# A written-out plan of 1175 operations drawn up anew: orders, engines and slots of a fused attention and gMLP kernel

## The chip, the cores and the metric

The kernel runs on one core of one Trainium2 chip. The core has a matrix engine (TensorE, PE in the profile; its weight loads are PEld), a vector engine (VectorE, DVE), an activation engine (ScalarE, ACT), a general engine (GpSimd, POOL) and a sequencer that issues transfers (SyncE, SP). Each engine works through its own list of instructions in order; semaphores make one wait for another. The metric is the time of one execution on the device in microseconds. The median of three runs is given, and one execution has been recorded by the hardware profiler.

## The reference, cut to what matters

```python
def _A_ref(x, wqkv, wo):          # S = 2048 rows, D = 448, H = 16 heads of 28, window W = 256
    q, k, v = ...                 # x @ wqkv, split in heads
    scores = jnp.einsum('bhqd,bhkd->bhqk', q, k) * Dh ** (-0.5)
    mask = (idx[:, None] - idx[None, :] >= 0) & (idx[:, None] - idx[None, :] < W)
    p = _softmax(jnp.where(mask[None, None], scores, -1000000000.0), axis=-1)
    return jnp.einsum('bhqk,bhkd->bhqd', p, v) ... @ wo

def _B_ref(x, w_in, w_sp, b_sp, w_out):
    z = _gelu(jnp.einsum('bsd,df->bsf', x, w_in))          # 1792 columns
    z1, z2 = z[..., :Fh], _layernorm(z[..., Fh:])          # Fh = 896
    g = jnp.einsum('ts,bsf->btf', w_sp, z2) + b_sp[None, :, None]
    return jnp.einsum('bsf,fd->bsd', z1 * g, w_out)

sa, ca, ga, sb, cb, gb = ...                               # silu(c) @ w_mod, six rows of 448
h = _layernorm(x) * (1 + ca) + sa
x = x + ga * _A_ref(h, A_wqkv, A_wo)
h = _layernorm(x) * (1 + cb) + sb
x = x + gb * _B_ref(h, B_w_in, B_w_sp, B_b_sp, B_w_out)
```

Everything is bf16; sums of products are kept in float32.

## The kernel before, in words

The 2048 rows are 16 tiles of 128 rows, in four blocks of four tiles. All data stays in on-chip memory between the load of x and the store of the result. The work is described as 1175 operations. An operation is one instruction, or for PE a short run of matmuls into the same bank of PSUM, or one transfer. Each has the engines that may do it (`ways`), the operations that it depends on (`deps`), and the buffers that it takes (`take`): a slot of a small rotating buffer or one of eight PSUM banks.

Nothing is scheduled while the program is built. The string PLAN holds one word per operation, in one order for all engines. In the word `a402.5` the letter names the engine (p PE, a ACT, d DVE, t POOL, s SP), the number the operation, and what follows the slots that it takes. `Sched.order` reads the words one after another. Each engine's own list is its words in that order; whoever takes a slot waits for all users of what held it before. Then the semaphores are counted and the waits written in front of the instructions. So PLAN alone says which engine does an operation, what stands ahead of it on that engine, and which buffer it has to wait for.

The stages, with the lines that the text names:

- **Start.** x and the first weights are loaded by SP and ACT (L395, L398, L404, L408). PE forms c's column (L515) and the rows sa and ca (L545, words p45 to p48); DVE copies them to modT (L574, L575, words d85 and d86). The 36 matmuls of L564 are fillers on a constant tile whose result nobody reads. For the first block the layer norm is statistics (L628, L630, DVE), the power of the variance (L632, POOL) and xn (L643, DVE; words d116, d117 for the first two tiles). PE transposes xn (L739), and DVE or ACT moves it out of PSUM to hT, multiplied and shifted by modT (L748 is ACT's form, L750 DVE's; words 126, 127, 129, 130 for the first two tiles). WQK is a padded copy of the weights of q and k in eight parts (L616 on DVE or POOL, L617 on ACT; word d106 is one).
- **Later blocks.** xn is made by DVE or POOL (L643, or L648 and L650), SP issues one transposing transfer per tile (L465, hT<-xn; words s193 to s196 for the second block), and hT is multiplied and shifted in place (L731).
- **Projections.** L796, L820 and L762 form q and k from WQK, L840 forms v; they are moved out of PSUM by ACT (L801, L771, L832, L844) or DVE (L802, L772, L833, L845). q is also copied into a block-diagonal tile QBD, in pieces (L814, L789 on ACT; L815, L790 on DVE). Operation 217 is the first L820 of the second block.
- **Attention of tile j.** Scores (L925 for the first two tiles, then L955 and L966), exponentials on ACT (L911), masks by multiplication on DVE (L974, L995), products with v (L1002), the reciprocal of the sum and its product on DVE (L1016, L1018), a transposing transfer (hT<-o_sb), the product with wo (L1028, scaled by POOL or DVE in L600) and the sum with x (L1032, DVE). Operation 775 is an L1002 of the last tile but one.
- **Second layer norm.** L628, L630, L632, L643 or L648 and L650, a small copy (L655, L656), a transposing transfer (hT<-xn, the second use of that name) and the multiplication (L1051 on ACT, L1053 on DVE or POOL).
- **gMLP.** L1122 and L1143 are the products with w_in, with gelu on ACT (L1129, L1151), z2 is normalized (L628, L630, L632, then L1134 on DVE). L1167 is the product with w_sp, 28 groups of 16 matmuls of 512 columns: each is followed by an addition on DVE (L1171) and a product on POOL (L1174). L1186 is the product with w_out, L1196 the sum with x on DVE, L1201 the store. w_sp comes in by 32 transposing transfers (wspA, wspB).

Inside an engine's list nothing overtakes. A transfer waits at the head of SP's list for its input, and everything behind it in that list waits as well.

The lines that turn a word into a place on an engine and a buffer:

```python
for at, word in enumerate(PLAN.split()):
    n, *slots = map(int, word[1:].split("."))
    op = self.ops[n]
    for h, k in zip(op.take, slots):
        h.slot = h.res.options[k]
        for u in h.slot:
            old = h.res.last[u]
            if old is not None:
                op.deps.update(old.until)
            h.res.last[u] = h
    op.eng = names[word[0]]
    self.prog[op.eng].append(op)
```

Of the kernel before, what the change touches and what calls it, by code (L numbers as in the profile page):

```python
# [15 lines left out]
d126 d127 d120 d121 d118 d119 a107 p83.1 p80.0 p81.1 p79.2 p77.0 p55.3 p72.2 p71.0 s12 d183 d181 p65.1 t104  # L16
p54.0 p149.1 p84.2 p140.5 p141 p150 a151 p82.1 p57.2 a142 t109 t110 t108 p137.7 p138 a139 p66.2 t122 d124.2
d123.0 p134.3 p131.6 p69.3 p56.0 p146.0 p147 p61.2 a132 d177 d184 d135 a136 s13 d243 d179 d178 d182 d180 t28
t185 t191 t187 t189 d245 d44 d241 d186.3 s11 p143.7 p370.0 a133 p164.1 p171.6 p172 d244 p165 d166 a148 p152.0
p144 d145 d173 d247 p153 d154 a371.0 p376.0 p155.1 p156 d157 a42 a377.4 p394.0 a395.1 a396 a170 t39 d380 d372  # L20
d246 d167 d374 p158.7 p159 a160 s15 p93.1 p94 d95 d248 d87 d88 d242 d397 p96.0 p97 d98 d378 s193 t188.1 s194
t190.2 s195 t192.0 s196 d197 d200 p401.0 a402.5 p174.1 p175 a176 p161.7 p162 p373.0 p89.0 p90 d91 d198 d92
a403 a43 p421.0 a422.6.0 t249 t253 d404 t251 t199 p375 p379 p381 d406 d382 d399 t252.2 d163 p217.0 p218 a219
a169 p210.1 p211 d212 p429.0 a430.0 p201.0 p202 a203 d168 p204.1 p205 a206 s14 d309 d383.2 p398.0 p400 p448.0
a449.2.1 s16 d426 s831 s258 t254.1 s259 d250.0 d255 d425 d432 d311 s384 s257 t256.3 s260 t100 t99 t261 t102
t262 t264 p226.0 p423.0 a424 p207.1 p227 p405 p208 d228 d305 p407 d408 d409.1 d306 s410 d101 d310 d431 a209
d215 d453 p456.0 p229.0 a457.1 d459 d214 d458 d452 p220.1 p221 p230 a231 p427.0 p428 s833 p475.0 p433 p434
d435 p223.0 p224 d225 d312 p450.0 a222 p232.1 d436.2 s437 d213 a476.3.2 d480 p483.0 d307 p233 d234 p235.0 p236
a451 a216 p477.0 p454.0 p455 a484.0 p501.0 d485 d486 d308 s21 s17 s834 p460 p461 d462 d479 d463.0 s464 a237
t263 p385.0 p386 d387 p411.1 p412 a478 p503.0 d413 t313 a502.6.0 p528.0 a504 d388 d505 d389 p481.0 p482 p487  # L30
p488 p271.0 p530.0 d489 d490.1 a529.2.1 d533 d506 d532 p272 a273 p509.0 a510.5 p268.1 p274.0 p275 d276 p269
d270 p507.0 p508 a531 p555.0 a556.3.2 p281.0 p265.1 p266 a267 d512 p282 p557.0 a558 a283 d511 p513 t317 t318.1
s323 t319 t320.2 s324 d314.0 s321 t315 t316.3 s322 t328 d279 d414 d560 p536.0 a537.1 p438.1 p439 d440 d280
p514 d515 d516.0 p287.0 p288 a289 p290.1 p291 a292 p563.0 a564.5 p238.0 p239 d278 p293.1 p534.0 p294 p535
p582.0 a240 p465.0 p466 d441 d442 d538 d415 d277 s20 s491 s830 s517 t390 d539 d391.2 t392 s393 a295 a583.4.0
d559 p540 p541 p284.1 p584.0 p285 a286 p590.0 a591.2 d566 d467 p299.0 p300 a301 d542 d543.1 p561.0 p562 d586
d565 d468 p567 p568 p608.0 t416 t327 t325 d326 d587 p518.1 p335.0 p519 d569 d570.0 p588.0 a585 p589 p336 d593
# [10 lines left out]
d578 t579.2 d746 d655 p721.0 p722 p727 p750.0 a751.4 p728 d747 d729 d730.1 s731 p360.1 p361 p625.0 p744.0 p626
p769.0 d752 d627 d753 d628 a362 p748.0 p679.1 p680 d681 a745 p749 p754 p755 d756 d757.2 p771.0 a770.6.0 p777.0
a772 p706.1 p707 p732.0 p733 d773 d774 p775.0 p776 t580 s581 t809 a778.1 p852.0 p853.1 p854 d656 d708 d734  # L50
d779 d682 d780 d808 t604 d605.0 s758 p759.0 p760 d761 p781 p782 d783 d784.0 a856 d629 t630 t631 p855 a862
p868.3 p869.2 p870 p871 a878 a872 p980.0 p981.1 p982 p983 a986 a987 d735 d736 t657 t658 t606 t659.2 d857 d683
t810 t807 p884.3 p885.2 p886 p887 d709 d710 d632.1 d762 d763 d879 d633 s369 s825 s785 s826 s607 t684 d685 s634
a984 a985 p900.0 p901.1 p902 p903 t737 t711 t660 d686.0 t687 a894 d895 d896 t764 a888 p996.3 p997.2 p998 p999
s661 d712.1 d858 d738 s688 s840 s824 s823 a904 p988.0 d905 a814 a910 p989.1 p990 a1000 a1001 a1003 a992 a1002
a993 p786.0 t799 t797 t713 t811 t813 t801 t812 d765 d889 t766.0 d859 d863 d874 d906 s714 d864 t767 s768 d907
t739.2 d897 d912 t898 d865 d880 d890 p787 d788 d740 s741 s832 p991 a995 d789 d790 t791 d873 d911 d875 t792
d793.1 p932.2 a994 p933.0 p934 p935 a936 d937 p916.1 p917.3 a942 d944 d938 d943 d913 p918 a920 d922 p919 a926
p1004.0 p1005.1 p1006 p1007 a1011 a1009 a1010 a1008 t860 t794 s795 t818 d817 t816 d891 d815 d881 d939 d927
d899 d928 d945 t914 t876 d877 d921 t908 d909 t882 d923 p948.2 p949.3 p950 p951 p964.1 p965.0 p966 a952 d929  # L60
d953 d954 a958 d959 d955 d883 d960 t892 t956 d893 t940 p967 a968 a974 p1028.3 p1029.1 p1030 p1031 t866 t930
t946 t924 t800 a1032 a1033 p1012.2 p1013.3 p1014 a1034 p1020.0 a1035 p1021.1 p1022 p1015 a1017 a1016 a1018
a1025 p1023 a1026 a1027 a1019 a1024 d976 d961 d970 d975 d969 d977 d931 d971 t978 d861 d915 d925 d941 d947 d979
d867 s828 s822 s827 s829 s820 s844 s821 s851 s845 s850 t972 d973 d957 t962 d963 p1087.4 p1051.5 s819 p1036.1
d1037.1 d1088.0 t1038 p1048.2 p1090.4 t1089 p1042.7 d1043.0 t1044 d1049.0 t1050 p1081.3 d1082.0 t1083 s839
s836 s838 s849 s841 s843 s846 s837 s847 s842 s848 p1123.7 p1072.2 d1124.0 d1052.1 t1053 t802 t796 t1125
p1120.0 d1121.1 t1122 p1084.7 d1085.1 t1086 p1156.3 d1157.1 t1158 d1073.1 t1074 d1091.1 p1078.6 p1138.7
d1079.0 t1080 t1092 p1045.4 p1039.6 d1046.1 p1153.1 t798 t1047 d1040.0 t1041 d1139.0 p1075.6 p1114.2 p1054.4
p1141.0 p1150.7 d1055.1 t1056 d1076.1 p1060.4 p1147.6 t1077 p1096.5 t1140 d1154.0 p1144.1 d1061.3 d1115.1
p1093.2 d1097.0 t1155 d1145.0 p1102.3 p1063.1 p1057.4 t1146 d1142.0 s1098 d1103.0 t1116 p1105.5 s1062 d1151.1  # L70
d1094.3 t1152 d1058.2 s1059 d1148.1 t1149 d1106.1 t1107 p1069.4 d1070.1 s1071 d1064.1 s1095 s1065 p1108.7
p1117.5 p1111.0 d1109.1 t1110 d1112.1 t1143 p1167.2 p1066.1 t1113 p1163.4 d1118.0 t1119 s1104 d1067.0 s1068
p1168 d1169.0 s1170 p1171.0 p1172 d1173.2 s1174 p1126.3 p1129.6 d1130.0 d1127.1 s1128 s1131 p1159.5 p1160
p1164 d1161.3 s1162 p1099.2 d1165.0 d1100.2 s1101 s1166 p1132.5 d1133.3 s1134 p1135.3 d1136.1 s1137
# [1194 lines left out]
```

## Time and profile before

| | us |
|---|---|
| median of three runs | 277.24 |
| lowest and highest | 277.05, 278.53 |
| the profiled execution | 277.96 |
| its span on the core | 276.2 |
| PE, DVE, ACT, POOL busy | 268.5, 163.7, 121.5, 118.1 |

The profile gives each instruction's start and length on each engine. Busy is the part of a stretch in which at least one instruction of the engine runs. A group of instructions is named by its line, its engine, its operation and what it writes and reads; "us, mean ns" is the time of all and of one. A wait is named by the group that waited and the group that ended it, with the sum, the number and the longest. The chain is found by following back, from the last instruction, what released each step. The granted clock is 1.00 at full speed and 0.50 at half.

### The profile page before, as it was taken

What the parts mean: (1) busy time and instruction counts of PE and PEld (TensorE: products, weight loads), DVE (VectorE), ACT (ScalarE), POOL (GpSimd) and SP (SyncE); (2) the same over time, 40 slices, a digit from 0 to 9 for tenths busy, and PEclk for the clock granted to TensorE, in tenths of its full rate; (3) what the DMA queues carried; (4) which work ended last, traced back from release to release, by engine and by line L of the source; (5) the groups of instructions that cost most, each with busy time, mean ns of one, the idle gap of its engine ahead of it and who ended that gap; (6) DMA issues with size and microseconds to landing.
All of it is one profiled execution on the core that took longest, in us unless ns stands there. A gap on an engine that the chain in (4) does not pass through costs nothing.

```text
span 276.2 us, 8403 instructions
## 1 busy us (share of the span) xinstructions
PE 268.5 (97%) x3751; PEld 155.1 (56%) x3751; DVE 163.7 (59%) x365; ACT 121.5 (44%) x142; POOL 118.1 (43%) x160
## 2 busy tenths in 40 slices
PE   7999998999999899999999999999999999999995
PEld 5976686678677676544444444444444444454552
DVE  3799999979899989939789301221212022153143
ACT  2599998899899689476766500000000000000000
POOL 7565467626574231498258003254453023062320
PEclk9999999999999799999999999999999999999999
DMA  7999744845442533658499996000000000001013
GB/s 206 316 221 189 96 101 114 107 96 110 114 63 61 107 60 61 176 114 141 97 155 191 213 182 135 0 0 0 2 0 0 0 2 0 33 17 63 0 39 116
DMA packets 67301, 25.54 MB, mean 92 GB/s; under 512 B 58497, under 2 KB 66178, under 8 KB 67266
## 3 DMA queue, kind: packets, MB, share of 16 engines
q1 hardware_dynamic: 66304, 24.21, 43.8%
q10 hardware_dynamic: 962, 0.80, 1.1%
q8 instruction: 29, 0.48, 0.8%
q14 instruction: 6, 0.05, 0.1%
HBM read 9.01 MB, written 1.84 MB: 39 GB/s over the span
## 4 chain that ended last, share of the span: by engine, by line
PE 78%; DVE 13%; DMA 4%; POOL 1%; SPq 1%; issue 1%; DVEq 0%
PE ps L1167 35%; PE ps L1122 8%; PE ps L1143 8%; PE ps L1186 8%; PE ps L1002 5%; DVE PT L974 4%; PE ps L1028 4%; PE ps L955 3%; DMA x_sb<-in_A_x_dram 3%; PE ps L820 3%; PE ps L762 2%; DVE st_all L628 2%; PE ps L840 2%; DMA hT<-xn 2%; DVE o_sb L1018 1%
## 5 line engine op out<-in xcount | busy, mean ns | idle before, releaser
L1174 POOL TENSOR_TENSOR z1T<-tmpg,z1T 128x512 bf16<-128x512 bf16 x28 | 32.0, 1153 | 77.2 <-DVE tmpg L1171 77.2
L1171 DVE TENSOR_TENSOR tmpg<-ps,bsp_bc 128x512 bf16<-128x512 f32 x28 | 19.0, 689 | 76.0 <-PE ps L1167 64.7
L911 ACT ACTIVATE PW<-ps 128x2048 bf16<-128x2048 f32 (+1 forms) x42 | 59.9, 1451 | 6.1 <-PE ps L955 4.5
L1167 PE MATMUL ps<-wspB,z 128*128 128x512 bf16 x224 | 50.1, 379 | 0.0
L1167 PE MATMUL ps<-wspA,z 128*128 128x512 bf16 x224 | 49.5, 379 | 0.0
L632 POOL TENSOR_TENSOR rs_all<-mv_all,neghalf 128x1 f32<-128x1 f32 (+2 forms) x37 | 24.1, 672 | 34.3 <-DVE mv_all L630 34.3
L974 DVE TENSOR_TENSOR PT<-PW,mask 128x1024 bf16<-128x1024 bf16 x56 | 38.0, 702 | 0.2
L1167 PEld LDWEIGHTS ps<-wspA,z 128*128 128x128 bf16 x224 | 21.8, 98 | 26.6 <-issue 0.4
L1167 PEld LDWEIGHTS ps<-wspB,z 128*128 128x128 bf16 x224 | 21.9, 98 | 26.2
L1002 PE MATMUL ps<-Vaug,PT 128*128 128x32 bf16 x496 | 23.3, 177 | 1.4 <-DVE o_sb L1018 1.4
L1002 PEld LDWEIGHTS ps<-Vaug,PT 128*128 128x128 bf16 x496 | 21.4, 96 | 4.3 <-DVE o_sb L1018 2.2
L1122 PE MATMUL ps<-w_in,hT 64*128 64x448 bf16 x224 | 22.0, 350 | 0.0
L1186 PE MATMUL ps<-w_out_g,z1T 128*128 128x448 bf16 (+2 forms) x119 | 22.0, 342 | 0.0
L1143 PE MATMUL ps<-hT,w_in 64*128 64x512 bf16 x196 | 22.0, 376 | 0.0
L628 DVE BATCH_NORM_STATS2 st_all<-z 128x6 f32<-128x448 bf16 x32 | 18.4, 606 | 5.8 <-ACT z L1129 5.8
L628 DVE BATCH_NORM_STATS2 st_all<-x_sb 128x6 f32<-128x448 bf16 x32 | 19.4, 615 | 2.9 <-DMA x_sb<-in_A_x_dram 2.7
L1002 PE MATMUL ps<-Vaug,PW 128*128 128x32 bf16 x224 | 19.7, 177 | 0.0
L820 PE MATMUL ps<-hT,WQK 112*128 112x128 bf16 x256 | 17.9, 223 | 1.6 <-DVE KT L833 1.1
L1151 ACT ACTIVATE z1T<-ps 128x512 bf16<-128x512 f32 x28 | 14.6, 603 | 9.1 <-PE ps L1143 9.1
L1196 DVE TENSOR_TENSOR fin<-ps,x_sb 128x448 bf16<-128x448 f32 (+2 forms) x17 | 9.8, 595 | 14.7 <-PE ps L1186 9.9
L1002 PEld LDWEIGHTS ps<-Vaug,PW 128*128 128x128 bf16 x224 | 17.6, 96 | 1.1
L1129 ACT ACTIVATE z<-ps 128x896 bf16<-128x896 f32 x16 | 13.9, 913 | 7.9 <-PE ps L1122 5.4
(105 smaller groups left out, 354.1 us busy)
## 6 DMA issues: line engine op xcount, KB each, us to landing
out_dram<-fin SPq DMA_DIRECT2D x15, 112.0 KB, 1.7
wmodB<-in_w_mod_dram SPq DMA_DIRECT2D x1, 1568.0 KB, 15.0
x_sb<-in_A_x_dram SPq DMA_DIRECT2D x3, 448.0 KB, 8.0
w_in<-in_B_w_in_dram SPq DMA_DIRECT2D x3, 448.0 KB, 4.5
w_out_g<-in_B_w_out_dram SPq DMA_DIRECT2D x1, 784.0 KB, 4.7
bsp_bc<-in_B_b_sp_dram SPq DMA_DIRECT2D x1, 512.0 KB, 5.1
x_sb<-in_A_x_dram SPq DMA_DIRECT2D x2, 224.0 KB, 4.8
hT<-xn SPq DMA_TRANSPOSE x28, 3.2
```

Of the source, the lines that this page charges most:

```text
L628: st = [dve(0.62, lambda e, t=t, o=12 - 6 * (n - ci), s=s: e.bn_stats(st_all[:, slot, t, o:o + 6], s()), deps(t), prio) for ci, s in enume ...
L632: return pool(0.4 + 0.15 * len(tiles), lambda e: e.tensor_tensor(rs_all[:, slot, a:b], mv_all[:, slot, a:b, 1], neghalf[:, 0:b - a], ALU.pow),
L820: km = lambda g, kc, start, stop, h=h, t=t: lambda e: e.matmul(ps[:, h.slot[0], g * 128:(g + 1) * 128], lhsT=WQK[0:CP, kc, 16 + 4 * g:20 + ...
L911: ex = act(xdur, lambda e, out_ap=out_ap, in_ap=in_ap: e.activation(out_ap(), in_ap(), ACT.Exp, scale=SCALE), [s] + list(after), v - 8.0 + ...
L974: return lock_d(0.68, lambda e: e.tensor_tensor(cols(hp.slot[0] * 2048 + 1024 * k, [[256, 4], [128, 2], [1, 128]]), cols(at_w() + pad + at ...
L1002: fns.append(lambda e, hp=hp, hO=hO, hi=hi, bi=bi, kb=kb, hd=hd, nb=nb, a=at[hi][bi], p_of=p_of: e.matmul(ps[:, hO.slot[0], 32 * hd:32 * h ...
L1122: return lambda e, kc, p0, start, stop: e.matmul(ps[:, hs[t % 2].slot[hf], 0:D], lhsT=hT[p0:p0 + 64, kc, t * 128:(t + 1) * 128], rhs=w_in[ ...
L1143: return lambda e, kc, p0, start, stop: e.matmul(ps[:, hs[b // 2].slot[b % 2], :], lhsT=w_in[p0:p0 + 64, kc, ft * 128:(ft + 1) * 128], rhs ...
L1167: m = pe(16 * MMS, [lambda e, h=h, si=si, ft=ft, tb=tb: e.matmul(ps[:, h.slot[0], :], lhsT=z2[:, si, ft * 128:(ft + 1) * 128], rhs=(wspA i ...
L1171: a = dve(0.7, lambda e, h=h, ht=ht, tb=tb: e.tensor_tensor(tmpg[:, ht.slot[0], :], ps[:, h.slot[0], :], bsp_bc[:, tb * 512:(tb + 1) * 512 ...
L1174: u = pool(1.16, lambda e, ht=ht, ft=ft, tb=tb: e.tensor_tensor(z1T[tb][:, ft, :], tmpg[:, ht.slot[0], :], z1T[tb][:, ft, :], ALU.mult), [ ...
L1186: return [lambda e, ft=ft: e.matmul(ps[:, h.slot[0], 0:hi - lo], lhsT=z1T[t // 4][:, ft, (t % 4) * 128:(t % 4 + 1) * 128], rhs=w_out_g[:, ...
```

## The change

Only PLAN is replaced. The operations, their tiles and sizes, and what they depend on by data are the same 1175. Three things differ: the order of the words, the letter of some words (the engine), and the slots and banks behind the dots. The first lines of the diff, and some of its last:

```diff
 PLAN = """
-d24 d22 p50.1 p59.3 p51.2 p58.0 p60.1 p62.0 a0 a3 a5 a7 a9 d23 d25 d26 d27 p40.1 p68.2 p74.3 p64.1 p52.0 p67.2
-p53.3 p76.0 p49.3 p70.0 s1 s2 s4 d113 s6 s10 s8 a41 p45.0 p46 p47.1 p48 p73.2 p75.1 p63.2 t30 t31 t32 t35 t36
-t33 d111 d114 t34 d112 t115 t37 a103 t29 t105 t38 d117.3 d116.2 p125.7 d86 d85 p128.0 p78.0 a129 a130 d106
...
+t33 t34 d23 d25 t36 t30 a0 a3 d24 d27 p40.1 p72.0 a5 a7 p49.0 a9 s1 p58.0 p56.2 p61.0 s2 s4 a41 s6 d111 d113
+t31 s10 d26 s8 d114 p66.0 d112 p59.1 p51.0 p50.3 p71.0 p45.1 p46 p77.0 p73.1 p54.1 d85 t115 t28 t32 d116.3
+d106 p52.0 p47.1 a105 d117.0 p48 d86 p125.7 p128.5 p80.2 d126 p64.2 p60.0 p62.0 p69.1 t104 t103 a127 t109 d129
...
-d1094.3 t1152 d1058.2 s1059 d1148.1 t1149 d1106.1 t1107 p1069.4 d1070.1 s1071 d1064.1 s1095 s1065 p1108.7
...
+d1067.0 s1098 s1104 d1070.3 d1112.1 p1171.0 p1117.5 p1167.4 p1163.3 p1172 s1068 d1118.0 p1168 t1113 t1119
```

66 operations change their engine. By kind: from ACT to DVE four evictions of hT (L748), three of q (L771), two of k (L832), one of v (L844), two copies into QBD (L789, L814); from DVE to ACT six copies into QBD (L790), three evictions of q (L772, L802), two of v (L845), two of hT (L750), one multiplication of hT (L731); from POOL to DVE six xn (L650), five L648, three small copies (L656), two multiplications of hT (L731), two scalings of wo (L600), one L1053; from DVE to POOL five L648, two L655, two L1053; from POOL to ACT seven L1053, two copies to WQK, one L731; from ACT to POOL one L1051 and one copy to WQK. The 36 fillers of L564 are kept: 29 of them stood ahead of the first L820, now 22 do. On PE the order of the long groups differs by small exchanges; on SP the transfers of the second block are issued as s195, s196, s193, s194 instead of s193 to s196.

More of the change, by code (lines that the diff above doesn't have):

```diff
@@ L18 @@
[L18 to L37, printed above, removed]
@@ L48 @@
[L48 to L52, printed above, removed]
```

91 lines of the change are left out of this document (58 added, 33 removed).

## The prediction

> **What bounds the kernel now.** I read the page first, then the chain that ended last, then the busy time of each engine in stages cut where the chain changes its engine. 10.06 is the first useful matmul (L820), 27.49 the first matmul of the second block of 512 rows (plan word p217), 109.40 an L1002 of the last row tile but one (p775), 155.07 the first L1167, 260.74 the end of the last L1167.
>
> ```profile
> span 276.2 us, 8403 instructions
> PEclk9999999999999799999999999999999999999999
> ...
> 0.00:10.06 10.06, 8.46 (x73) 6.39 (x74) 4.43 (x18) 3.08 (x5) 7.11 (x19) 1.00 0.85 233
> 10.06:27.49 17.43, 16.86 (x311) 13.10 (x312) 15.96 (x46) 15.18 (x21) 9.55 (x18) 1.00 1.18 234
> 27.49:109.40 81.91, 79.47 (x2324) 58.17 (x2325) 77.22 (x163) 72.17 (x71) 38.84 (x46) 0.98 0.50 90
> 109.40:155.07 45.67, 45.67 (x478) 22.28 (x476) 37.63 (x97) 28.54 (x43) 27.59 (x48) 1.00 0.77 147
> 155.07:260.74 105.67, 105.67 (x500) 48.67 (x499) 21.53 (x33) 2.50 (x6) 32.71 (x29) 1.00 0.17 37
> 260.74:276.20 15.46, 12.40 (x70) 6.45 (x68) 6.94 (x12) 0.00 (x0) 2.27 (x2) 0.99 0.21 69
> ```
>
> The columns after the length are PE, PEld, DVE, ACT and POOL busy, then the granted clock. From 109.40 to 260.74 PE is busy without a gap: there a new order can only lose. The stage 27.49 to 109.40 is different. PE 79.47, DVE 77.22 and ACT 72.17 of 81.91 us are three nearly full engines that wait for each other, and here PE lost time in three places:
>
> ```profile
> PE ps L1002 <- DVE o_sb L1018: 1.4, 1, 1.4
> PE ps L820 <- DVE KT L833: 1.1, 1, 1.1
> ...
> 40.44:43.85 3.41, 2.36 (x70) 1.64 (x69) 3.41 (x8) 3.13 (x4) 3.41 (x4) 1.00 0.22 46
> 88.22:91.64 3.42, 2.03 (x79) 1.80 (x67) 3.42 (x9) 2.42 (x3) 3.01 (x7) 1.00 0.50 142
> 91.64:95.05 3.41, 3.41 (x100) 2.95 (x97) 3.09 (x8) 1.88 (x2) 0.00 (x0) 0.50 0.46 105
> ```
>
> Both waits are for DVE, together 2.5 us. After the second, PE ran 3.41 us at half clock, which costs half of that, 1.7 us. So PE alone would have needed 81.9 - 2.5 - 1.7 = 77.7 us for this stage, no more than DVE's 77.2: the two bound it together.
>
> **The change part by part.** Every operation stays; only the 1175 words of PLAN change. I follow four times through it.
>
> *Start, up to p217.* Before, the first useful matmul waited for copies of WQK and for evictions of hT:
>
> ```profile
> 7.99 0.56 POOL L616 COPY WQK<-wq_st 112x448 bf16<-112x448 bf16 x1 [1.47 <-DMA wq_st<-in_A_wqkv_dram]
> 8.13 0.55 DVE L616 COPY WQK<-wq_st 112x448 bf16<-112x448 bf16 x1
> 8.56 1.36 PE L564 MATMUL ps<-fill 128*128 128x256 bf16 x11
> 8.62 0.86 DVE L750 TENSOR_SCALAR hT<-ps,modT 112x256 bf16<-112x256 bf16 x2
> 10.06 0.61 PE L820 MATMUL ps<-hT,WQK 112*128 112x128 bf16 x8
> ```
>
> Now DVE does its copy (d106) ahead of the second xn (d117), for which the transposes on PE wait. The copy's input lands at about 7.95 (POOL's wait ends at 7.99), so d117 ends near 8.9 (8.0 + 0.55 + 0.4), the transposes near 9.4, and three instead of two evictions stand on DVE (d126, d129, d130; 0.43 each) to 10.6, one on ACT. The first useful matmul moves from 10.06 to about 10.3. Behind it now stand 14 fillers instead of 7: seven by 1.36/11 = 0.12 are 0.8 us more on PE, which the wait for the next item covers.
>
> That item is the transposing loads of the second block, and p217 waits for them:
>
> ```profile
> 15.49 1.02 POOL rs_all L632
> ...
> 19.79 1.22 SPq L465
> 21.05 4.35 DMA hT<-xn
> 25.43 1.12 DVE hT L731 x2
> ...
> 27.49 1.05 PE ps L820 x16
> ...
> 17.10 6.13 SPq L465 DMA_TRANSPOSE hT<-xn  x4
> ```
>
> SP issued four, the first at 17.10 (of the tile that DVE normalized), one per 1.3 us, the last at 21.05, which landed 4.35 later. Now the tile that POOL normalizes second in its list after L632, a mask (L508) and an L648 goes first (word s195 ahead of s193). L632 starts at about 15.9, since the DVE evictions above come ahead of its last statistics (0.4 later than 15.49). It takes 1.0, then 0.3 + 0.3 + 0.7 us of POOL: SP starts at 18.2, 1.1 later. The last lands at 26.4 instead of 25.40. Three L731 on DVE follow, 0.55 each, where it took 2.06 us with others between them: p217 at about 28.3. **Term: +0.8 us.** Ends: 0 (the loads come earlier than now) and +1.1 (all of SP's lateness).
>
> *27.49 to 109.40.* Between the last DVE word that p217 waits for and the one for p775, DVE takes sixteen from others (three L772, two L833, one L845 from ACT; four L650, two L600, two L648, one L731, one L655 from POOL) and gives fifteen (six L790, two L772, two L845 to ACT; three L648, one L655, one L1053 to POOL). Four short ones of its own (L995, L643, two L630; 1.1 us) now also stand here.
>
> ```profile
> L790 DVE COPY QBD<-qT 32x512 bf16<-32x512 bf16 x11 | 3.5, 321 | 1.5 <-ACT qT L771 1.3
> L772 DVE CAST qT<-ps 128x512 bf16<-128x512 f32 x4 | 2.7, 689 | 1.0 <-PE ps L762 1.0
> L845 DVE CAST Vaug<-ps 128x448 bf16<-128x448 f32 x4 | 2.4, 607 | 0.0
> L833 DVE CAST KT<-ps 128x512 bf16<-128x512 f32 x2 | 1.3, 646 | 0.0
> ...
> L650 DVE TENSOR_SCALAR xn<-x_sb,rs_all,nm_all 128x448 bf16<-128x448 bf16 x4 | 1.9, 470 | 0.0
> L731 DVE TENSOR_SCALAR hT<-hT,modT 112x512 bf16<-112x512 bf16 x4 | 2.2, 586 | 0.7 <-DMA hT<-xn 0.7
> L600 DVE TENSOR_TENSOR wo_g<-wo_g,gg_sb 112x448 bf16<-112x448 bf16 x1 | 0.6, 600 | 0.0
> ```
>
> The first four rows are of this stage alone, the others of the whole run. Taken: 3 x 0.69 + 2 x 0.65 + 0.61 + 4 x 0.47 + 2 x 0.60 + 0.59 + 1.0 (the small ones, by 0.2 and 0.6) = 8.6. Given: 6 x 0.32 + 2 x 0.69 + 2 x 0.61 + 1.7 (small ones and L1053, by 0.2, 0.6 and 0.5) = 6.2. With the 1.1 the net is +3.5, less 0.1 for each of the five instructions more, as neighbours overlap (the pair at 37.90 below takes 1.29, not 2 x 0.70): +3.0, so DVE 80.2. ACT gains the six copies and two multiplications of hT and gives evictions of about 0.6 each: some +3.5, so 75.7. POOL loses about 7 of its 38.8.
>
> Less POOL means less disturbance of DVE:
>
> ```profile
> 37.90 1.29 DVE L974 TENSOR_TENSOR PT<-PW,mask 128x1024 bf16<-128x1024 bf16 x2
> 39.23 0.75 DVE L790 COPY QBD<-qT 32x512 bf16<-32x512 bf16 x1
> 40.01 2.02 DVE L974 TENSOR_TENSOR PT<-PW,mask 128x1024 bf16<-128x1024 bf16 x2
> ...
> 38.96 0.87 POOL L731 TENSOR_SCALAR hT<-hT,modT 112x512 bf16<-112x512 bf16 x1 [2.57 <-DMA hT<-xn]
> 39.80 1.07 POOL L600 TENSOR_TENSOR wo_g<-wo_g,gg_sb 112x448 bf16<-112x448 bf16 x1
> ```
>
> While POOL ran L731 and L600, one copy took 0.75 instead of 0.32 and one pair 2.02 instead of 1.29: 1.2 us lost, and it is these that made PE wait 1.1 us for KT. How much such loss the whole stage holds no row says; a seventh to a fifth of POOL's work leaves, and I take 0.4 back: DVE 79.8. [...]
>
> To these 79.8 us comes what DVE idles. Now it idles 81.91 - 77.22 = 4.7 us; ends: nothing (79.8, 2.1 less than now) and 4.7 (84.5, 2.6 more). Where DVE is the last, it hardly idles (all 3.41 us of 40.44:43.85 and 3.42 of 88.22:91.64 are busy); I take half of today's, 2.3: 82.1. **Term: +0.2 us.** PE would be done in 77.7 and ACT's 75.7 fit too, so DVE becomes the bound here, with PE's waits spread.
>
> *109.40 to 155.07.* One L1028 pair (p733) moves from ahead of p775 to behind it:
>
> ```profile
> 97.16 0.38 PE ps L1028 x2
> L1174 POOL TENSOR_TENSOR z1T<-tmpg,z1T 128x512 bf16<-128x512 bf16 x28 | 32.0, 1153 | 77.2 <-DVE tmpg L1171 77.2
> L1171 DVE TENSOR_TENSOR tmpg<-ps,bsp_bc 128x512 bf16<-128x512 f32 x28 | 19.0, 689 | 76.0 <-PE ps L1167 64.7
> ```
>
> PE has no gap to absorb it: **+0.4 us**. DVE has 8.0 us of room here, and the last normalizations of z stand, as before, behind the same last gelu.
>
> *155.07 to the end.* The L1167 groups change places; PE stays full if the last one's result arrives in time. Its addition and product (0.69 + 1.15, and about 0.2 of passing on) take 2.05 us; fourteen L1186 matmuls of 0.19 (half of the pair above) lie between, 2.65. **0**; if that cover were gone, at most the 2.05.
>
> Sum: 0.8 + 0.2 + 0.4 = **+1.4 us** on the profiled execution (277.96, of which 276.2 is the span), so 279.4. The median of the runs is 277.24, 0.7 lower; the forecast for a median is 277.24 + 1.4 = **278.6 us**.
>
> **The rivals.**
> (1) *DVE goes on waiting.* ACT too is fuller, 75.7, and DVE waits for ACT today (1.3 us of L790's idle). If DVE idles 4.7 us as now, the stage takes 84.5: +2.6 instead of +0.2, total +3.8, **281.0**. Against it: an engine that becomes the bound idles less.
> (2) *An early half clock.* A stretch with 2.03 of 3.42 us busy was followed by half clock, one with 2.36 of 3.41 was not. In the changed order the stretch 6.30 to 9.72 holds the later L545 matmuls, 4 fillers, the 8 transposes (waiting for d117 until 8.9) and some of the 8 fillers behind them, an estimated 2.1 to 2.6 us by the rows of the start. If the clock halves for 9.72 to 13.13, about 1.4 us more: +2.8, **280.0**. [...]
> (3) *Faster, the other side: DVE packs tightly.* If DVE idles nothing and PE no longer stalls long enough for a half clock, the stage is 79.8 and the total -2.1 + 0.8 + 0.4 = -0.9; with p217 no later (term 0), -1.7, **275.5**. It decides when DVE's idle falls under 1 us. For it: the two waits of PE are single places, both could go. Against it: DVE's own 3.0 us more.
> (4) *It does little.* L820 to L1028 keep nearly their order on PE, and the exchanges cancel: **277.3**.
>
> **How the numbers follow.** Forecast 0.38, (1) 0.25, (2) 0.10, (3) 0.20, (4) 0.07. A measurement of this kernel tells about 0.5% (1.4 us) from no change. The forecast lies on that edge, half same, half slower (0.19 each). Slower: 0.19 + 0.25 + 0.09 = 0.53; faster: 0.17 of (3); same: the rest, 0.30. The range leaves out a tenth on each side: low 275.5, the far end of (3); high 281.6, above (1) by half a microsecond for what (2) may add.
>
> **What would show it.** The first L820 after 10.06, near 10.3; p217's L820 at about 28.3 with the transposes landing near 26.4; DVE busy about 80 of some 82 us between p217 and p775 and more waits of PE on DVE, none longer than now; POOL busy some 7 us less there; the first L1167 near 156.5 and 118 us from it to the last matmul. Wrong would be: a granted clock of 0.5 near 10 (rival 2), DVE idle over 4 us (1) or under 1 (3), or a PE gap after the first L1167.

## The result, and the profile after

| | before | after |
|---|---|---|
| median of 20 executions each, us | 277.98 | 279.86 |
| lowest and highest | 276.58, 280.55 | 278.47, 282.22 |
| ratio after to before, 95% interval | | 1.0068, 1.0043 to 1.0092 |
| profiled execution: time, span | 277.96, 276.2 | 279.06, 277.3 |

The changed kernel is slower, by 0.7% or 1.9 us. The forecast was 1.4 us (278.6 against a base of 277.24).

First the head of the page after, then its busy times in stages cut at the same instructions as before: the first L820 (now at 10.55), p217 (28.92), p775 (109.59), the first L1167 (156.36), the end of the last L1167 (263.47). The columns after the length are PE, PEld, DVE, ACT, POOL busy and the granted clock.

```profile
span 277.3 us, 8395 instructions
PEclk9999999999999999999999999999999999999999
```

```profile
0.00:10.55 10.55, 7.79 (x66) 6.52 (x67) 3.87 (x17) 2.43 (x4) 5.34 (x16) 1.00 0.86 241
10.55:28.92 18.37, 17.54 (x308) 13.06 (x307) 17.04 (x50) 16.28 (x24) 10.01 (x18) 1.00 0.82 192
28.92:109.59 80.67, 78.75 (x2334) 57.12 (x2335) 76.86 (x167) 75.82 (x76) 32.63 (x41) 1.00 0.55 96
109.59:156.36 46.77, 46.34 (x479) 22.43 (x480) 38.01 (x97) 32.24 (x48) 22.75 (x39) 1.00 0.77 141
156.36:263.47 107.11, 106.64 (x501) 49.62 (x510) 22.08 (x35) 2.00 (x5) 33.65 (x30) 1.00 0.22 38
```

Against before, p217 comes 1.43 us later (10.06 + 17.43 = 27.49 became 28.92), the stage to p775 is 1.24 shorter (81.91), the next 1.10 longer (45.67), and from the first L1167 to the last matmul it is 117.89 in place of 118.07. The half clock of the profile before (0.98 for that stage, with 0.50 for 3.41 us) is gone: the clock of every stage is 1.00. In the waits of PE between p217 and the first L1167 the two on DVE (1.4 and 1.1 us) are gone as well; what stands there now is this:

```profile
PE ps L1028 <- issue: 0.9, 1, 0.9
PE ps L955 <- ACT PW L911: 0.7, 2, 0.5
PE ps L1167 <- DVE z L1134: 0.4, 1, 0.4
```

"issue" is a stop for which the profile shows no reason. It turned out to be the most instructive line of the page.

One pair of profiles doesn't make a table of stages. The experiments below repeat the words of both plans stage by stage, and so show how far one execution scatters. Lengths in us, from the first instruction of each stage; a bracket marks a stage whose words were edited:

| profile | to first L820 | to p217 | to p775 | to first L1167 | to last matmul |
|---|---|---|---|---|---|
| before | 10.06 | 17.43 | 81.91 (half clock) | 45.67 | 118.07 |
| old start, new rest | 11.10 | 16.78 | (81.76) | 46.54 | 118.81 |
| old, clearing late | 10.10 | (17.44) | 81.34 | 45.66 | 118.07 |
| old, DVE order | 10.38 | 16.78 | (82.28) | 45.67 | 118.07 |
| old, w_in together | 10.81 | 16.78 | (81.21) | 45.67 | 118.07 |
| after | 10.55 | 18.37 | 80.67 | 46.77 | 117.89 |
| new start, old rest | 9.64 | 18.74 | (81.58) | 45.67 | 118.07 |
| new, old behind p775 | 11.33 | 18.34 | 80.83 | (46.05) | 118.07 |
| new, w_sp load moved | 10.06 | 18.50 | (82.22) | 46.53 | 118.92 |
| new, w_in load moved | 10.04 | 18.42 | (80.85) | 46.52 | 118.63 |
| new, clearing early | 10.13 | (17.32) | 81.21 | 46.54 | 118.13 |
| new, three words | 10.38 | (17.55) | (83.37, half clock) | (46.30) | 118.34 |
| new, four words | 10.15 | (17.31) | (83.69, half clock) | (46.26) | 118.67 |
| new front, old back | 10.05 | (17.60) | (80.68) | (46.04) | 118.07 |

The first column scatters by 1.7 us under the same words. In two profiles that both have the old start, PE waited 0.2 us for the first weights (wmodA, before) and 1.2 (old start, new rest), and the first L820 came at 10.06 and 11.10. The second scatters by 0.7 us at most and the fourth hardly, and there the two plans stand apart. The last is 118.07 in all seven profiles with the old order there, and 117.89 to 118.92 in the seven with the new one. The half clock is the exception: 97 executions of the old plan ran beside the experiments, and 19 had a mean granted clock under 0.9965; comparisons leave out nine that were more than 1.5% longer than the fastest, and of the other 88, 12 had such a mean (median 278.83 us) and 76 hadn't (277.39). The profile on which the prediction rested had one as well (0.993).

### The profile page after: what moved, and what is told of

The parts are those of the page before. It is cut to its first block, busy times and chain, and to the rows that moved or that the text cites. A ratio compares the mean times of both kernels' runs of the same rounds, so it can differ in the third digit from the quotient of the medians.

```text
span 277.3 us, 8395 instructions
## 1 busy us (share of the span) xinstructions
PE 267.8 (97%) x3741; PEld 154.1 (56%) x3751; DVE 163.8 (59%) x373; ACT 128.8 (46%) x152; POOL 105.5 (38%) x142
## 4 chain that ended last, share of the span: by engine, by line
PE 76%; DVE 15%; ACT 5%; DMA 1%; issue 1%; POOL 1%; SPq 0%; DVEq 0%
PE ps L1167 35%; PE ps L1186 8%; PE ps L1002 5%; PE ps L1122 5%; DVE st_all L628 5%; PE ps L1028 4%; PE ps L955 4%; ACT PW L911 4%; PE ps L1143 3%; PE ps L820 3%; PE ps L840 3%; DVE z L1134 2%; PE ps L762 2%; DVE PT L974 2%; DMA wmodA<-in_w_mod_dram 1%
## 5 line engine op out<-in xcount | busy, mean ns | idle before, releaser
L1171 DVE TENSOR_TENSOR tmpg<-ps,bsp_bc 128x512 bf16<-128x512 f32 x28 | 18.7, 688 | 69.5 <-PE ps L1167 52.9
L632 POOL TENSOR_TENSOR rs_all<-mv_all,neghalf 128x1 f32<-128x1 f32 (+2 forms) x37 | 24.1, 659 | 67.5 <-DVE mv_all L630 67.4
L1167 PE MATMUL ps<-wspB,z 128*128 128x512 bf16 x219 | 49.4, 379 | 0.3
L1167 PE MATMUL ps<-wspA,z 128*128 128x512 bf16 x219 | 48.6, 379 | 0.6 <-DVE z L1134 0.4
L1167 PEld LDWEIGHTS ps<-wspA,z 128*128 128x128 bf16 x224 | 21.8, 98 | 26.9 <-DVE z L1134 0.7
L1167 PEld LDWEIGHTS ps<-wspB,z 128*128 128x128 bf16 x224 | 21.9, 98 | 26.0
L1002 PE MATMUL ps<-Vaug,PT 128*128 128x32 bf16 x496 | 24.7, 177 | 0.1
L1002 PEld LDWEIGHTS ps<-Vaug,PT 128*128 128x128 bf16 x496 | 22.2, 96 | 4.4 <-DVE PT L974 1.2
L1122 PE MATMUL ps<-w_in,hT 64*128 64x448 bf16 x224 | 22.9, 349 | 0.0
L1143 PE MATMUL ps<-hT,w_in 64*128 64x512 bf16 x196 | 22.6, 376 | 0.0
L1196 DVE TENSOR_TENSOR fin<-ps,x_sb 128x448 bf16<-128x448 f32 (+2 forms) x17 | 9.6, 594 | 21.4 <-PE ps L1186 16.3
L1002 PE MATMUL ps<-Vaug,PW 128*128 128x32 bf16 x224 | 20.6, 176 | 0.0
L820 PE MATMUL ps<-hT,WQK 112*128 112x128 bf16 x256 | 17.9, 219 | 0.1
L955 PE MATMUL ps<-qT,KT 32*128 32x128 bf16 (+5 forms) x1344 | 17.1, 197 | 0.9 <-ACT PW L911 0.7
```

What stands on the lines that cost most here:

```text
L632: return pool(0.4 + 0.15 * len(tiles), lambda e: e.tensor_tensor(rs_all[:, slot, a:b], mv_all[:, slot, a:b, 1], neghalf[:, 0:b - a], ALU.pow),
L820: km = lambda g, kc, start, stop, h=h, t=t: lambda e: e.matmul(ps[:, h.slot[0], g * 128:(g + 1) * 128], lhsT=WQK[0:CP, kc, 16 + 4 * g:20 + ...
L955: fm.append(lambda e, hm=hm, qi=qi, key=key, kn=kn, lo=lo, hi=hi, col=col, p0=p0, t=t, j=j: e.matmul(ps[p0:p0 + kn, hm.slot[t], col:col + ...
L1002: fns.append(lambda e, hp=hp, hO=hO, hi=hi, bi=bi, kb=kb, hd=hd, nb=nb, a=at[hi][bi], p_of=p_of: e.matmul(ps[:, hO.slot[0], 32 * hd:32 * h ...
L1122: return lambda e, kc, p0, start, stop: e.matmul(ps[:, hs[t % 2].slot[hf], 0:D], lhsT=hT[p0:p0 + 64, kc, t * 128:(t + 1) * 128], rhs=w_in[ ...
L1143: return lambda e, kc, p0, start, stop: e.matmul(ps[:, hs[b // 2].slot[b % 2], :], lhsT=w_in[p0:p0 + 64, kc, ft * 128:(ft + 1) * 128], rhs ...
```

## Experiments

The theory after the comparison: the start loses because POOL clears Vaug (L499) beside the two xn of DVE; PE's unexplained stop is its own code arriving late; the end of the third stage loses because POOL scales w_out (L1044) beside the last normalizations of z. The first rival: the stages aren't independent, and what one gains or loses the next gives back. The ratios are to the old plan, with 95% intervals, from 11 or 12 executions of each kernel (six of the one with the old start and of the two that move a single load in the new plan) and one profile. In the first four kernels every line number of the code is one lower than elsewhere (L642 for L643).

### Are the stages independent? Exchanging the starts

```diff
-(the new plan's words up to p217.0) d406 d399 d397 ...
+(the old plan's words up to p217.0) (the new plan's other words, in its order)
```

> The words up to p217 are those of the old plan, the rest stands as in the new plan. Profiles of old and new: first block-two matmul (p217) at 27.49 and 28.92 us, so the new start costs 1.43; from p217 to p775 the new plan takes 80.67 where the old took 81.91. Theory S (the start is lost for good, the later stages stand by themselves): p217 near 27.5, stage to p775 near 80.7, and the time 1.4 us under the new plan's, near 0.2 to 0.5 us from the old one (ratio to the old 0.998 to 1.002). Rival C (catching up: the new plan's 1.24 us in the second stage is only the late p217 made up, because DVE and ACT set the pace and go on working while PE waits): p217 near 27.5, stage to p775 near 82, ratio to the old the same as that of the new plan, 1.005 to 1.008.

```diff
-(the old plan's words up to p217.0) p218 a219 ...
+(the new plan's words up to p217.0) (the old plan's other words, in its order)
```

> The words up to p217 are those of the new plan, the rest stands as in the old plan: the other half of the pair. Theory S: p217 near 28.9, stage to p775 near 81.9, ratio to the old plan 1.005 (1.4 us more). Rival C: p217 near 28.9, stage to p775 near 80.5, ratio 1.000 to 1.002.

Measured: 281.13 us and 1.0105 (1.0058 to 1.0151) with the old start, 280.03 us and 1.0084 (1.0049 to 1.0119) with the new one. Neither theory gave that: both halves are slower than the old plan, and neither is faster than the new one. The table shows that p217 moved as theory S has it (16.78 and 18.74 us behind the first L820), but the stage behind the seam is 81.76 and 81.58. The words ahead of p217 aren't the same set in both plans: the old start holds eight operations more, nearly all of the first tiles' attention (163, 375, 379, 381, 382, 397, 399, 406), the new one two loads and three small operations (14, 16, 168, 169, 255). What one start leaves undone the other's rest doesn't expect. With the old start PE now waits for o_sb (0.9 us) and for an exponential (0.9 us), waits that neither whole plan has there at that size. So a plan can't be judged by exchanging halves at p217; the single words below can.

### POOL beside DVE in the start

In the profile after (first fence DVE, second POOL) the two xn take 1.82 us where the old plan took 0.69, while POOL clears Vaug; L643 ends behind the clearing (14.38), not beside it:

```profile
12.99 1.82 DVE L643 TENSOR_SCALAR xn<-x_sb,mv_all,rs_all 128x448 bf16<-128x448 bf16 x2 [0.32 <-POOL rs_all L632]
```

```profile
13.15 1.23 POOL L499 MEMSET Vaug<- 128x768 bf16 x1
```

The next normalization waits for them, first POOL's variance of the second block, then SP's transfers of it:

```profile
17.24 1.01 POOL L632 TENSOR_TENSOR rs_all<-mv_all,neghalf 128x4 f32<-128x4 f32 x1 [2.58 <-DVE mv_all L630]
```

```profile
19.60 6.06 SPq L465 DMA_TRANSPOSE hT<-xn  x4
```

```diff
-d85 t115 t28 t32 d116.3 ... p68.0 t37 t35 t38
+d85 t115 t28 t32 t35 d116.3 ... p68.0 t37 t38
```

> The new plan with one word moved: t35, POOL's clearing of Vaug (L499, 1.23 us), stands right behind t32, where POOL waits for wq_st from 6.3 to 8.6 us, in place of beside the two xn (L643) at 12.99, which took 1.82 us together (0.69 in the old plan). Theory M (POOL beside DVE costs the start 1.1 us): the two L643 take 0.7 to 0.8, L632 of the second block starts near 16.1 instead of 17.24, SP's first transposing transfer near 18.5 instead of 19.60, p217 near 27.8; ratio to the old plan 1.002 to 1.004, 0.8 to 1.1 us under the new plan's. Rival E (the evictions and the order on DVE set it): L643 shorter, but p217 stays at 28.5 or later, ratio to the old plan 1.006 to 1.008.

Measured: 279.36 us, 1.0060 (1.0028 to 1.0091). In its profile, DVE, POOL twice and SP:

```profile
12.52 0.72 DVE L642 TENSOR_SCALAR xn<-x_sb,mv_all,rs_all 128x448 bf16<-128x448 bf16 x2 [0.31 <-POOL rs_all L631]
```

```profile
6.43 1.22 POOL L498 MEMSET Vaug<- 128x768 bf16 x1
```

```profile
15.68 1.01 POOL L631 TENSOR_TENSOR rs_all<-mv_all,neghalf 128x4 f32<-128x4 f32 x1 [2.56 <-DVE mv_all L629]
```

```profile
18.04 1.30 SPq L464 DMA_TRANSPOSE hT<-xn  x1
```

The pair takes 0.72, the variance (L632 elsewhere) starts at 15.68 in place of 17.24, SP at 18.04 in place of 19.60, and p217 comes at 27.45. In four profiles with the clearing early p217 stands 17.3 to 17.6 us behind the first L820, in five with it late 18.3 to 18.7. Counted from the variance (L632) of the first block's last two tiles, that of the second block starts 3.9 us later in the four and 5.0 in the five, to within 0.02. Theory M is right about the mechanism and its size on p217, 1.0 us. The time fell by less than a measurement tells; this profile has the unexplained stop at 1.5 us in place of 0.9, so a part was given back there.

So xn is held up beside the clearing, an instruction of POOL that only writes: in the profile after, the first L643 took 1.52 us (12.99 to 14.51) in place of 0.39 and ended 0.13 us behind the end of the clearing, which took 1.23 beside it and 1.22 without. It was held up whichever of the two started first: here L643 had started 0.16 us ahead of the clearing, in the next trial 0.14 us behind it. By what, the traces don't show.

The reverse, in the old plan:

```diff
-t31 t32 t35 t36 ... d180 t28 t185
+t31 t32 t36 ... d180 t28 t35 t185
```

> The old plan with one word moved: t35, POOL's clearing of Vaug, stands behind t28, so that it runs beside the two xn (L643) at 12.49, as in the new plan. The reverse of the trial that moved it out of the new plan. Theory M: the two L643 take 1.8 us in place of 0.69, L632 of the second block and SP's transposing transfers come 1.0 us later, p217 18.4 us behind the first L820 in place of 16.8 to 17.4, and the time rises by 0.7 to 1.1 us, ratio 1.003 to 1.004. Rival D (a late p217 is made up for by p775): p217 late, ratio 1.000 to 1.001. In the same profile the stage p217 to p775 of the old plan is seen once more; without a half clock it should take about 80.2 us, not 81.9.

Measured: 278.40 us, 1.0017 (0.9982 to 1.0052). One xn took 1.22 us in place of 0.39, and L632 started 0.6 later than in the profile before. p217 stands 17.44 behind the first L820: as in the profile before, but 0.7 later than in the other three with the old start (16.78). From the start of the span it comes at 27.54, in those four at 27.16 to 27.88. So the slowing shows in the old plan too, with half the size; how much of it reaches p217 there stays open, and the time tells nothing. The profile gives the old plan's second stage without a half clock:

```profile
27.54:108.88 81.34, 78.78 (x2332) 57.51 (x2328) 77.71 (x163) 72.93 (x72) 38.34 (x47) 1.00 0.52 93
```

81.34 where I had expected 80.2: the half clock of the profile before had cost the stage about 0.6 us, not 1.7.

### The end of the third stage

```diff
-(the new plan's words up to p775.0) p733 d779 d682 ...
+(the new plan's words up to p775.0) (the old plan's other words, in its order)
```

> The new plan up to p775, behind it the words of the old plan. Profiles: from p775 to the last matmul the new plan takes 164.66, the old 163.74; 0.4 of the difference is the pair p733, which also here stands behind p775, and 0.44 is a gap of PE before the first L1167, which waits for the last normalization of z. Theory G (the gap belongs to the new plan's tail): no gap before the first L1167, first L1167 46.1 us behind p775, time 0.4 to 0.5 us under the new plan's, ratio to the old 1.004 to 1.006. Rival N (the gap is where the chain of normalizations falls by chance, or PE's work in the tail is merely differently counted): within 0.2 us of the new plan, ratio 1.006 to 1.008.

Measured: 279.32 us, 1.0050 (1.0017 to 1.0083), and the first L1167 46.05 us behind p775, without a gap: theory G, as expected. In the profile after (DVE, then POOL, then PE) the five last normalizations take 2.97 us beside POOL's L1044, and PE waits:

```profile
153.11 2.97 DVE L1134 TENSOR_SCALAR z<-z,mv_all,rs_all 128x896 bf16<-128x896 bf16 x5
```

```profile
153.95 1.04 POOL L1044 TENSOR_TENSOR w_out_g<-w_out_g,gg_sb 128x448 bf16<-128x448 bf16 x1
```

```profile
156.36 0.38 PE L1167 MATMUL ps<-wspA,z 128*128 128x512 bf16 x1 [0.44 <-DVE z L1134]
```

In the kernel of four words below, which has t800 at 150.12, the same five take less, and no gap stands ahead of the first L1167:

```profile
154.67 2.31 DVE L1134 TENSOR_SCALAR z<-z,mv_all,rs_all 128x896 bf16<-128x896 bf16 x5
```

That stage is 46.30 and 46.26 with t800 early, 46.52 to 46.77 with it late: 0.25 to 0.5 us.

### PE's unexplained stop

In the profile after, the weights of an L1028 are loaded at 75.80; its matmul, which waits for no semaphore, starts 1.0 us later:

```profile
75.80 0.10 PEld L1028 LDWEIGHTS ps<-wo_g,hT 112*128 112x128 bf16 x1
...
76.80 0.54 PE L1028 MATMUL ps<-wo_g,hT 112*128 112x448 bf16 x2 [0.93 <-issue]
```

It is the 1750th matmul, and PE stops there, or two matmuls on, in every profile with these words (for 0.6 us with the old start, 0.9 to 1.5 in the others so far). The trace lists transfers of instructions on queue q8, 29 of 16 KB, about one per 128 of the 3741 matmuls; I take them for PE's code. One came at 74.49, 6.1 us after the one before in place of the usual 4, and PE went on 1.36 us after its end. First suspect, a load of w_sp:

```diff
-d326 s517 s491 a591.1 ... d494 t523 s830 s598
+d326 s517 s491 s830 a591.1 ... d494 t523 s598
```

> The new plan with one word moved on SP: s830, a transposing load of w_sp (wspA), is issued behind s491 (about 64 us) in place of behind s393 (72.19 us). In the new plan's profile, and in all three experiments that have its words there, PE stands still for 0.9 to 1.5 us between one weight load of L1028 and its matmul (at 75.8 to 76.8, the 1750th matmul each time) without a semaphore to wait for; the transfer of PE's instructions in front of it (16 KB, one per 128 matmuls) came at 74.49, 6.1 us after the one before it in place of the usual 4, while w_in and w_sp loads filled the queues from 70 to 76. Theory P (PE waits for its own code, which waits behind these loads): the code transfer comes near 72.5, no stop of PE at the 1750th matmul, the stage p217 to p775 0.9 us shorter (79.8 to 80.3), the time about 0.9 us under the new plan's, ratio to the old 1.002 to 1.005. Rival Q (the stop is something of that matmul's own): it stays at the same matmul, ratio unchanged at 1.006 to 1.008.

Measured: 280.71 us, 1.0106 (1.0062 to 1.0150), and the stop is still there, 1.2 us. This was the wrong load. The same edit stood in the next one:

```diff
-d85 t115 t28 t32 d116.3 ... s491 a591.1 ... s830 s598 ... t898 p1014 ... d909 t800
+d85 t115 t28 t32 t35 d116.3 ... s491 s830 a591.1 ... s598 ... t898 t800 p1014 ... d909
```

> The new plan with three words moved: t35 (clearing of Vaug on POOL) behind t32, s830 (load of w_sp) behind s491, t800 (scaling of w_out on POOL, L1044) behind t898, where POOL idles, in place of beside the last normalizations of z, where one L1134 took 1.16 us in place of 0.46 and the first L1167 waited 0.44. If each costs by itself and PE has no other wait to put in its place: 1.1 + 0.9 + 0.4 = 2.4 us under the new plan's time, ratio to the old 0.996 to 1.001; in the profile p217 17.3 us behind the first L820, no stop at the 1750th matmul, no gap before the first L1167. Rival (each gap closed is opened again by the next engine in line, as DVE and ACT are nearly full): ratio to the old 1.003 or more.

Measured: 279.42 us, 1.0061 (1.0031 to 1.0091). p217 and the first L1167 came as expected, but PE stopped for 2.1 us at the 1750th matmul, and a half clock followed (0.50 from 77.29 to 80.71). The code again came right behind the last rows of two loads of w_in that stand one behind the other on SP (s19, s17), which fill the queues from 71 to 75 us. In the profile after, the transfers between 70 and 78 us:

```profile
DMA  0000088989899999988999990007000999990006
...
q8 instruction: 2, 0.03, 1.7%
...
w_in<-in_B_w_in_dram SPq DMA_DIRECT2D x2, 448.0 KB, 4.6
```

```diff
-p568 d569 p608.0 s19 a301 ... p723.0 s500 s20 t804
+p568 d569 p608.0 a301 ... p723.0 s500 s20 s19 t804
```

> The new plan with one word moved on SP: s19, a load of 448 KB of w_in, is issued behind s20 (about 96 us; w_in is first used at 110.7) in place of directly ahead of s17, the next load of w_in. Moving s830 left the stop of PE at the 1750th matmul where it was (1.2 and 2.1 us), with the transfer of PE's code again at 74.7 to 75.1, right behind the last large rows of the two w_in loads (896 KB, 71 to 75 us). Theory P2 (these two loads together hold the code transfer back): one load of 448 KB is through by 73, the code transfer comes near 72.5 to 73, the stop is gone or under 0.3 us, the stage p217 to p775 takes 79.6 to 80.1 us, the time 0.9 us under the new plan's, ratio to the old 1.002 to 1.005. Rival X (the code transfer keeps its place whatever the loads do): the stop stays at 0.9 or more, ratio 1.006 to 1.008.

Measured: 280.47 us, 1.0124 (1.0067 to 1.0181), from six executions. The code now came at 73.03, and of the stop 0.23 us was left. But a new one stood at the 2516th matmul, six pieces of code on, behind the load that I had moved:

```profile
75.34 1.29 PE L1028 MATMUL ps<-wo_g,hT 112*128 112x448 bf16 x6 [0.23 <-issue]
```

```profile
102.22 0.39 PE L955 MATMUL ps<-qT,KT 32*128 32x32 bf16 x26 [0.72 <-issue]
```

The stop follows the load, which is theory P2's mechanism; its sum failed, since the moved load took the stop along. Why this kernel and the one with s830 moved are no faster than the new plan stays open; their intervals overlap with its.

```diff
+(the kernel of three words, and) p568 d569 p608.0 a301 ... p723.0 s500 s20 s19 t804
```

> The new plan with four words moved: t35, s830 and t800 as in the trial of three, and s19 as in the trial of the one load. The trial of three had a ratio of 1.006, with p217 17.5 us behind the first L820, no gap before the first L1167 and a stop of PE of 2.1 us at the 1750th matmul. If the stop goes and nothing takes its place: 0.9 to 2 us less, ratio 0.999 to 1.003. Rival (DVE and ACT, 77 and 76 of 81 us busy, hold the stage at its length): the stop goes, PE waits elsewhere between p217 and p775, that stage stays at 81 or more, ratio 1.004 to 1.006.

Measured: 279.45 us, 1.0050 (1.0010 to 1.0089). Stops of 0.7 us at the 1750th and 1.3 at the 2516th matmul, and again a half clock behind the second (0.50 from 102.80 to 106.22). In its profile the 1.0 us won ahead of p217 is lost in the second stage, which took 83.69. The rival of both kernels of several words has the total right, though in these profiles by another way: not DVE and ACT, but PE's code and the half clock behind it.

The counter-trial in the old plan:

```diff
-p546 s18 p594 ... d613 s835 s571 ... d672 s19 p641.0
+p546 p594 ... d613 s835 s18 s19 s571 ... d672 p641.0
```

> The old plan with two words moved on SP: s18 and s19, two loads of w_in, stand one behind the other behind s835 (about 69 us), as s19 and s17 do in the new plan. Taking them apart in the new plan moved the stop of PE from the 1750th matmul to the 2516th, six pieces of code on, behind the moved load. Theory P2 (PE's code waits behind the rows of w_in): the code transfer that comes at 72.08 in the old plan comes at 74 to 75, PE stops at the 1750th matmul, which it reaches at 74.65, for 1 to 2 us, and the stage p217 to p775 grows from 81.3 (old plan's words, no half clock) to 82.3 to 83.3; ratio to the old plan 1.003 to 1.006. Rival Y (only the new plan's words have such a stop, from something else in them): code transfer near 72, no stop, ratio 1.000.

Measured: 277.80 us, 1.0030 (0.9989 to 1.0071). The code came at 73.24 in place of 72.08 and took 1.5 us, and a stop of 0.46 us appeared at the 1752nd matmul, which the old plan hadn't had. So the direction is right and the size a third of what was expected; the stage kept its length (81.21).

All fourteen profiles together say when such a piece hurts. It starts while PE does the 128 matmuls ahead of the 1750th, which take 3.3 to 3.8 us. Where the piece started 0.8 to 1.4 us behind the first of them (the profile before and three more with the old plan's order on PE there), PE lost 0.1 us at most. Where it started 1.3 to 3.2 us behind, PE lost 0.2 to 2.1 us, the later the longer in all but one. With the new plan's words the loss was 0.2 to 0.7 us with one load of w_in in front and 0.6 to 2.1 with two, so keeping them apart shortens this stop and doesn't end it.

### Two attempts at a faster kernel

The old plan, with DVE's order changed where PE waits for it:

```diff
-d459 d214 d458 d452 p220.1 ... p224 d225 d312 p450.0 ... s437 d213 a476.3.2
+d459 d214 p220.1 ... p224 d225 d452 p450.0 ... s437 d213 d458 d312 a476.3.2
...
-d304 d672 s19 ... d649 d805 t553 d650.0 s651 ... d353 a665
+d304 s19 ... d649 t553 d650.0 d672 s651 ... d353 d805 a665
```

> The old plan with five words of DVE moved, to close its two waits of PE: the mask d458 and the small d312 go behind d213 and d452 behind d225, so that KT of tile 5 (d225, L833) is moved out earlier, and L1053 (d805) goes behind d353 and the mask d672 behind d650, so that o_sb (d650) is ready earlier. Theory V (DVE's order sets these two waits): the wait of 1.05 to 1.3 us before operation 235 goes, that of 1.05 to 1.4 us before operation 668 falls under 0.4, the stage p217 to p775 takes 78 to 78.5 us, the time 1.5 to 2 us under the old plan's, ratio 0.993 to 0.995. Rival W (DVE as a whole sets the pace there: PE waits a few operations later for the words that were put back): the waits move behind 235 and 668, ratio 0.998 to 1.001.

Measured: 277.94 us, 1.0004 (0.9964 to 1.0043). Rival W: both waits went, and others of the same size came a few operations on, behind the words that were put back:

```profile
PE ps L955 <- DVE KT L833: 1.0, 1, 1.0
PE ps L966 <- DVE QBD L790: 0.8, 1, 0.8
PE ps L1002 <- DVE o_sb L1018: 0.7, 2, 0.4
```

And the new front with its two words mended, before the old back:

```diff
-... t32 d116.3 ... t37 t35 t38 ... p608.0 s19 a301 ... s20 t804 ... p775.0 (the new plan's rest)
+... t32 t35 d116.3 ... t37 t38 ... p608.0 a301 ... s20 s19 t804 ... p775.0 (the old plan's other words)
```

> The new plan up to p775 with t35 behind t32 and s19 behind s20, and behind p775 the words of the old plan. Sum of the stages as measured so far: first L820 10.3 (mean of six profiles), 17.4 to p217, 79.7 to p775 without the stop, 46.05 to the first L1167, 118.07 to the last matmul: 271.5, where the old plan without a half clock has 271.4 to 272.6. So it comes out level with the old plan or a little under it, ratio 0.997 to 1.001. Rival (the second stage is held by DVE and ACT): 81 or more from p217 to p775, ratio 1.003 to 1.006.

Measured: 278.75 us, 1.0032 (0.9998 to 1.0067). It wins back about half of what the change cost; its one profile adds up as expected in all stages but the second (80.68 in place of 79.7; PE still waits 0.4 us for its code and 0.5 for an exponential). No version beat the old plan.

## Why the prediction was right, and where its steps failed

The sum was near the result by errors of both signs, so its nearness is in good part luck. With the means of the table's untouched stages the change costs: first L820 -0.2 (10.26 against 10.49, within the scatter), on to p217 +1.5 (18.47 against 16.94), on to p775 -0.4 (80.90 against the one stage without a half clock, 81.34), on to the first L1167 +0.9 (46.58 against 45.67), the rest +0.4 (118.48, with the kernels of three and four words, against 118.07). That is +2.2; measured was +1.9, forecast +1.4.

- **Start, +0.8 forecast, about +1.3 shown.** The step "L632 starts at about 15.9" failed: it started at 17.24. I followed DVE's own list and SP's, and not what POOL does beside DVE: t35 stands there, and I had not looked where it went. With t35 out of the way (four profiles) L632 starts at 15.24 to 15.96 and SP at 17.60 to 18.33, around the 15.9 and 18.2 of the working. But that lateness hardly reached p217. From the start of the span p217 comes at 27.62 on average in these four, at 27.53 in the four profiles with the old start, and at 28.80 in the five with the clearing late. (From the first L820, which came 0.4 earlier in the four, it is 0.5 more than in the old plan.) So nearly all of the +1.3 is the clearing, which the working left out; of the 0.8 that it foresaw 0.1 is left, within the scatter, and that the two sizes lie near each other is luck. The first L820 waits for L545 and L575, not for d117; d106 has no visible price.
- **27.49 to 109.40, +0.2 forecast.** ACT was right (75.82, forecast 75.7), POOL nearly (6.2 less, forecast 7). "so DVE 80.2", and 79.8 with the contention, was wrong: 76.86. The 146 words of DVE that stand in this stage in both profiles took 80.1 us one by one before and 78.4 after: 1.7 less, which I put down to POOL's lighter load, where I took 0.4. The words taken less those given came to +2.9 (3.5 in the working), and neighbours overlap by 1.6 us more than before, not by 0.5. DVE idled 3.8, between the 2.3 assumed and the 4.7 of rival (1). It did not become the bound; PE's longest waits are its code and ACT.
- **The base.** The pair gives -1.24, but 0.6 of that is a half clock that 76 of 88 executions don't have. The 96 matmuls that ran at half clock took 3.53 us, in three profiles without it 2.46 to 2.64: it cost PE about 1.0 us, and "costs half of that, 1.7" was too much. I read one execution's accident as a property of the old plan, and rival (3) lived on it.
- **109.40 to 155.07, +0.4 forecast.** The moved pair p733 costs just that (46.05 and 46.04 against 45.67). What failed is the sentence that the last normalizations stand as before and have room: POOL's L1044 was moved beside them, 0.25 to 0.5 us. About 0.2 remains; PE changes 15 times between L1122 and L1143 there in place of 7, which wasn't tried.
- **155.07 to the end, 0 forecast.** Right in the profile after (-0.2), but 118.1 to 118.9 in the six others with the new order. PE waits for an L1196 there, 0.4 to 0.7 us in four of them (this is the trial that moved s830):

```profile
260.69 0.55 PE L1186 MATMUL ps<-w_out_g,z1T 128*128 128x448 bf16 x2 [0.68 <-DVE fin L1196]
```

That L1196 had had its products since 254.75 and started when a store had freed its slot of fin:

```profile
260.01 0.62 DVE L1196 TENSOR_TENSOR fin<-ps,x_sb 128x448 bf16<-128x448 f32 x1 [1.10 <-DMA out_dram<-fin]
```

I had worked out the cover for the addition and the product behind L1167, and not for the bank that L1196 still reads, nor for the stores that it waits for.

- **The early half clock of rival (2)** was not seen: in all fourteen profiles the granted clock is 1.00 from 9 us or earlier (6.30 before, 9.02 after) until far into the second stage. Rival (4) fell with the stages.

## What to carry to other kernels

When a schedule moves words on one engine, list what then runs on POOL beside each DVE instruction of the critical chain; two such places took 1.0 us of the way to p217 and 0.25 to 0.5 us ahead of the first L1167 here. Look for an "issue" wait of PE and for large loads in front of it: in this program of 8400 instructions the code came as transfers beside the data, and keeping two big loads apart shortened the stop, though part of it moved along with the load. Before a gain is counted, ask of a half clock in one profile how many executions have it.

## What the runs showed of the hardware

- **Code came late behind data.** Queue q8 of the profile after has 29 pieces of 16 KB. A piece that came late behind loads stopped PE for 0.2 to 2.1 us in the profiles here, and PE went on 1.1 to 1.5 us after the piece's end. Of the 29 pieces in the profile after one did so, that of 74.49, with a stop of 0.93 us.
- **Half clock.** Three profiles have a half clock between the first L820 and the last L1167, each of 3.41 us. With the span cut into stretches of that length which end where the granted clock changes, these stretches stand in front of them: that of the profile before, with 2.03 of 3.42 us of PE busy, and these two, from the kernels of three and of four words:

```profile
73.88:77.29 3.41, 1.27 (x66) 1.04 (x63) 1.75 (x4) 2.69 (x3) 2.66 (x5) 1.00 0.42 81
```

```profile
99.39:102.80 3.41, 2.14 (x75) 1.82 (x73) 3.41 (x9) 2.38 (x3) 2.06 (x3) 1.00 1.45 140
```

A stretch of the trial with the early clearing, with less busy time than two of them, was not followed by a half clock:

```profile
74.27:77.68 3.41, 1.91 (x33) 0.90 (x13) 2.11 (x5) 1.88 (x1) 1.85 (x4) 1.00 0.59 124
```

So the busy time alone doesn't decide it: 1.91 us in 3.41 had no half clock behind it, and 1.27, 2.03 and 2.14 had one.
